# One filter load moved in the DMA queue, one Newton chain on another engine, more output buffers: a spectral mixer with token MLP, forward and backward

## The chip, the cores and the metric

The kernel runs on one core of one Trainium2 chip. The metric is the device time of one execution in microseconds (us), lower is better. A core has five engines that work at the same time, each through its own queue of instructions in order: TensorE (PE in the profile; its weight loads are PEld), VectorE (DVE), ScalarE (ACT), GpSimd (POOL) and SyncE (SP). In this kernel SP issues every DMA transfer.

## The reference

A pre-norm block on x of 2048 tokens by 448 features, and the gradients of everything:

```python
h  = x + irfft2(rfft2(layernorm(x)) * (w_r + 1j * w_i))       # over tokens and features
h2 = h + transpose(gelu(layernorm(h)^T @ w1 + b1) @ w2 + b2)  # an MLP over the tokens
_out, _vjp = jax.vjp(_f, A_x, A_w_r, A_w_i, B_w1, B_b1, B_w2, B_b2)
_grads = _vjp(grad_out)
```

w1 is 2048 by 1792, w2 is 1792 by 2048, and the two filters w_r and w_i are 2048 by 225. Outputs are h2 and the gradients of x, both filters, both weight matrices and both biases.

## The kernel before

All big arrays stay in on-chip memory in named regions (`rA`, `rB`, ..., `rX`); a region is used for one thing after another. Small helper classes hand out buffers: a `Ring` is a list of views used in turn, and `Ring.next()` first issues a store that is still put off for the view it hands out. `defer(us, fn, views)` puts a DMA off by a number of microseconds of planned TensorE work. The order of the instructions on TensorE, VectorE, ScalarE and SP is the order in which the program writes them; GpSimd's alone is chosen by a scheduler. `evac`, which copies a matmul's result out, is given to ScalarE or VectorE by a planner's running sum of costs when the kernel is built.

**Stages.** The Fourier transforms are matrix products with sine and cosine tables that the kernel makes itself.

1. Rows of x (loop over 16 row tiles t, the loop `for t in range(NT)` near L860). `ln_stats` gives mean and variance of a tile, a Newton iteration gives the inverse square root (`rstd_x`), `scale_R` multiplies a small transform matrix by it, `fold_prep` adds and subtracts mirrored halves of two tiles, `row_a` and `row_b` are the two products of the transform. Every second tile ends with a reshuffle (the deferred DMA of L655 in `row_b`), which carries 226 KB from the partitions of the row layout to those of the column layout, `D2`. Eight reshuffles are made; the second transform needs all of them.
2. `s2_stage`, the transform over tokens: per group g three forward matmuls on `D2`, a complex product with the filter on VectorE (`w_mult`), three inverse matmuls (`s2_inv`). Six pairs of groups lie between a forward matmul and its inverse. The filter is loaded in raw form by `w_load` in eight transfers, four for w_r and then four for w_i (L571), and `w_place` copies it into place while the stage runs. The first transfer of each has 64 partitions by 3600 elements, 450 KB.
3. `inv_rows`, the transform back, with the second layer norm.
4. The MLP, its backward pass, then the same transforms backward with the two weight gradients as filling.

**Filling.** While a stage waits for other engines, TensorE is given matmuls of another product: `fill(n)` takes n matmuls from `pending`. In stages 1 and 2 this is `dg_gen`, w2 times the output gradient, in 14 blocks j of 16 matmuls. Each block needs a transposed load of w2 (`load_w2T`, L294, a DMA transpose into one of five buffers, three in `rE` and two in `rO`). Blocks 8 and later are held back and issued in `fwd_x(0)`, the start of stage 2, from a list of kinds: T is a held w2 transpose, W is the next filter transfer.

**Rows 4 and 5.** The inverse deviations of rows 0 to 3 come from ScalarE and VectorE. For rows 4 and 5 `newton_gp` (L844) writes ten GpSimd operations on 128 by 2 elements; the later groups, rows 6 to 15, use the same function from inside the loop. `newton` (L353) is the same iteration as a list of nine VectorE operations, wrapped by `rstd_of(a, b)`, which nothing called.

**The last stage.** The two weight gradients are made by `gw_gen` (L1203), first for w2 (14 blocks, right operand `goT` in `rG`), then for w1 (16 blocks). Two blocks at a time, two output buffers of 1024 columns each are taken twice, filled by four evictions and stored by a DMA each. All of them come from one ring, `ost` (L1200), of six buffers in `rO`. They are the filling of the backward transforms; what is left of them runs at the very end, after `inv_rows`. The gradient of x is stored row tile by row tile (L1293), that of the filters by `g_out` (L560), all on SP's one queue.

Of the kernel before, what the change touches and what calls it, by code (L numbers as in the profile page):

```python
# [17 lines left out]
P = 128  # L18
S = 2048
# [79 lines left out]
class Ring:  # L99
# [7 lines left out]
    def next(self):  # L107
        v = self.views[self.i % len(self.views)]
        self.i += 1
        Ring.release(v)  # L110
        return v
# [8 lines left out]
def kernel(  # L120
# [20 lines left out]
    nc = tc.nc  # L141
# [14 lines left out]
    def region(name, n):  # L156
        return mem.tile([P, n], BF16, name=name)

    def cut(reg, off, *dims):
        n = int(np.prod(dims))  # L160
        v = reg[:, off:off + n]
        if len(dims) == 1:
            return v
        names = "abcd"[:len(dims)]
        return v.rearrange("p (" + " ".join(names) + ") -> p " + " ".join(names),
                           **{c: d for c, d in zip(names, dims)})

    def ring(reg, off, count, *dims):
        n = int(np.prod(dims))
        return Ring([cut(reg, off + i * n, *dims) for i in range(count)])  # L170
# [57 lines left out]
    rG = region("rG", 4 * S)  # L228
# [34 lines left out]
    rstd_x = mem.tile([P, NT], F32, name="rstd_x")  # L263
# [4 lines left out]
    mvx = mem.tile([P, NT, 2], F32, name="mvx")  # L268
# [20 lines left out]
    def load_w2T():  # L289
        j = w2T_ring.i  # L290
        if j == NFB:
            return
        wT = w2T_ring.next()
        nc.sync.dma_start_transpose(out=wT, in_=B_w2[j * P:(j + 1) * P, :].rearrange("f (t c) -> f t c", c=P))  # L294
        w2Ts.append(wT)
# [57 lines left out]
    def newton(v, y, sl):  # L353
        vi, yi = nt_i[:, 0, sl], y.bitcast(I32)
        a = nt_f[:, 0, sl]
        ops = []
        d = Later(ve, ops)
        d.tensor_scalar(out=v, in0=v, scalar1=LN_EPS, scalar2=None, op0=ALU.add)
        d.tensor_scalar(out=vi, in0=v.bitcast(I32), scalar1=1, scalar2=None, op0=ALU.arith_shift_right)
        d.tensor_scalar(out=yi, in0=vi, scalar1=-1.0, scalar2=RSQRT_MAGIC, op0=ALU.mult, op1=ALU.add)  # L360
        for c0, c1 in RSQRT_STEPS:
            d.tensor_tensor(out=a, in0=y, in1=y, op=ALU.mult)
            d.scalar_tensor_tensor(out=a, in0=a, scalar=c0, in1=v, op0=ALU.mult, op1=ALU.mult)
            d.scalar_tensor_tensor(out=y, in0=a, scalar=c1, in1=y, op0=ALU.add, op1=ALU.mult)
        return ops

    def newton_gp(v, y, sl):
        vi, yi = nt_i[:, 0, sl], y.bitcast(I32)
        a = nt_f[:, 0, sl]
        gp_.tensor_scalar(out=v, in0=v, scalar1=LN_EPS, scalar2=None, op0=ALU.add)  # L370
        gp_.tensor_scalar(out=yi, in0=v.bitcast(I32), scalar1=-0.5, scalar2=RSQRT_MAGIC, op0=ALU.mult, op1=ALU.add)
        for c0, c1 in RSQRT_STEPS:
            gp_.tensor_tensor(out=a, in0=y, in1=y, op=ALU.mult)
            gp_.tensor_tensor(out=a, in0=a, in1=v, op=ALU.mult)
            gp_.tensor_scalar(out=a, in0=a, scalar1=c0, scalar2=c1, op0=ALU.mult, op1=ALU.add)
            gp_.tensor_tensor(out=y, in0=a, in1=y, op=ALU.mult)
# [374 lines left out]
    def fill(n):  # L751
        while n > 0 and pending:
            try:
                next(pending[0])
                n -= 1
            except StopIteration:
                pending.pop(0)
# [5 lines left out]
    def ln_stats(src, t, mv):  # L763
        ve.bn_stats(out=stats[:, t, :], in_=src[:, t, :])
        if t % 2:
            ve.bn_aggr(out=mv[:, t - 1, :], in_=stats[:, t - 1, :])
        if t % 2:
            ve.bn_aggr(out=mv[:, t, :], in_=stats[:, t, :])
# [30 lines left out]
    def rstd_of(a, b):  # L799
        return newton(mvx[:, a:b, 1], rstd_x[:, a:b], slice(a, b))  # L800
# [40 lines left out]
    fold_prep(xn, 1)  # L841
    for t in (4, 5):
        ln_stats(xn, t, mvx)
    newton_gp(mvx[:, 4:6, 1], rstd_x[:, 4:6], slice(4, 6))  # L844
    fill(6)
    turn_biases = load_biases()
    Meter.side, Meter.every, Meter.count = [], 1, 0
# [3 lines left out]
    for c in range(2):  # L851
        sc.copy(out=Rp.rearrange("p (a q b c) -> p c a q b", c=2, q=8, a=4)[:, c],
                in_=Rm[:, 64 * c:64 * c + 64].rearrange("p (q a b) -> p a q b", q=8, a=4))
    FILL_A = (3, 3, 3, 3, 3, 3, 3, 3, 3, 3, 3, 3, 3, 3, 3, 3)
    FILL_B = (3, 3, 3, 3, 3, 3, 3, 3, 3, 3, 3, 3, 3, 3, 3, 3)
    for t in range(NT):
        if t in (1, 3):
            load_w2T()
        if t + 1 < NT:
            row_a(t + 1, Rs.pop(t + 1))  # L860
        fill(FILL_A[t])
        if 1 <= t and t + 3 < NT:
            if t + 3 in (4, 8, 12):
                while Meter.side:
                    Meter.side.pop(0)()
            Rs[t + 3] = scale_R(t + 3)
        row_b(t - 1)
        if t == NT - 1:
            row_b(t)
        if t % 2 and t < 12:  # L870
            fold_prep(xn, t // 2 + 2)
        for i in STATS.get(t, ()):
            ln_stats(xn, i, mvx)
        for _ in range(3 if t > 0 else 0):
            if next(uv, None):
                break
        if t in GROUPS:
            a, b = GROUPS[t]
            newton_gp(mvx[:, a:b, 1], rstd_x[:, a:b], slice(a, b))
        for _ in range((9, 10, 11, 12).count(t)):  # L880
            next(w_loads)
        if t in INV_S:
            gen_inv_s(INV_S[t])
        if t in (13, 13 + 1):
            gen_neg((cut(r448, NG * P, 12, P), cut(rE, 3 * NT * P, 4, P))[t - 13], Ut[:, 12 * (t - 13):12 + 4 * (t - 13), :])
        if t == 2:
            gen_RT()
        fill(FILL_B[t])
# [5 lines left out]

    def fwd_x(c2):
        if c2 == 0:
            for kind in "TWWWWTTT":
                if kind == "W":
                    next(w_loads)
                elif held_w2:  # L900
                    held_w2.pop(0)()
            cap[0] = NFB
            while held_w2:
                held_w2.pop(0)()
        if c2 == 4:
            turn_biases()
        return Xs[:, 2 * c2:2 * c2 + 2, :, :]
# [256 lines left out]
    for t in range(NT):  # L1164
# [6 lines left out]
        pb, tmp, m1, m2, _ = ln_a(t, pdh[:, 0:D], rstd_h[:, t:t + 1], hln[:, t, :], (1.0 + LN_EPS) / D)  # L1171
# [28 lines left out]
    ost = ring(rO, 0, 6, S // 2)  # L1200
    o4 = out_4.rearrange("(p t) f -> p t f", t=NT)

    def gw_gen(n, rhs, width, store):  # L1203
        for u in range(n // 2):
            st = ahead.pop(0)

            def whole(pw, w, c, i, k, start, stop):
                mm(pw[i][:, 0:w], lhsT=st[:, 4 * i + k, :], rhs=rhs(c, k, 0, P), start=start, stop=stop)

            def parts(pw, w, c, start):  # L1210
                for i in range(2):
                    mm(pw[i][:, 0:w], lhsT=st[64 * i:64 * i + 64, 3, :], rhs=rhs(c, 3, 64 * i, 64 * i + 64),
                       start=start, stop=not start)

            def out(pw, w, c, i):
                o = os_[i]
                x = c % 2 * 512
                evac(out=o[:, x:x + w], in_=pw[i][:, 0:w])
                if x:
                    if c == 3 and i:  # L1220
                        st_load()
                    defer(1.5, lambda j=2 * u + i: store(j, 512 * (c - 1), x + w, o), o)

            for c in range(0, 4, 2):
                os_ = [ost.next(), ost.next()]
                pw = [ps_mm(), ps_mm()]
                for i in range(2):
                    for k in range(3):
                        whole(pw, 512, c, i, k, k == 0, False)
                        yield  # L1230
                w = min(512, width - 512 * (c + 1))
                pv = [ps_mm(), ps_mm()]
                parts(pw, 512, c, False)
                parts(pv, w, c + 1, True)
                for i in range(2):
                    out(pw, 512, c, i)
                yield
                yield
                for i in range(2):
                    for k in range(3):  # L1240
                        whole(pv, w, c + 1, i, k, False, k == 2)
                        if k == 2:
                            out(pv, w, c + 1, i)
                        yield

    pending.append(gw_gen(NFB, lambda c, k, a, b: goT[a:b, k, c * 512:(c + 1) * 512], S,
                          lambda j, a, n, o: nc.sync.dma_start(out=out_6[j * P:(j + 1) * P, a:a + n], in_=o[:, 0:n])))
    pending.append(gw_gen(NT, lambda c, k, a, b: du_t[a:b, 4 * c:min(NFB, 4 * c + 4), k, :], F,
                          lambda t, a, n, o: nc.sync.dma_start(out=o4[:, t, a:a + n], in_=o[:, 0:n])))
    nc.sync.dma_start(out=rC[:, 0:NG * 2 * KW], in_=w_d[:])  # L1250
    for t in range(NT - LAG, NT + 2):
        if t == NT - 2:
# [78 lines left out]
```

## Time and profile before

| | us |
|---|---|
| median of four runs | 369.52 |
| lowest and highest | 368.38, 369.76 |
| the profiled execution | 369.76 |
| its span | 368.0 |
| granted TensorE clock, mean | 0.994 of full |
| idle before TensorE's matmuls in rows 0 to 15 and the transform over tokens, longest after the start | 1.69, 1.40, 1.19 |

The span is the stretch from the first to the last recorded instruction; what lies around it is 1.76 us. A line of the timeline gives the start, the length, the engine, the source line, the operation, what it writes and reads, the number of instructions that are merged, and in brackets how long the engine stood before it and what ended that. The two helper lines, L215 (every matmul) and L79 (every planned vector or scalar operation), stand for many places in the program, so one goes by the names of the tiles.

### The profile page before, as it was taken

Reading aid. Unit: us, or ns where it says so; the run is one execution under the profiler, and the core shown is the slowest. Engines: PE = TensorE matmul, PEld = TensorE weight load, DVE = VectorE, ACT = ScalarE, POOL = GpSimd, SP = SyncE. Lnnn points to the kernel's source line nnn. Section 1 sums busy time; section 2 is a strip of 40 time slices with the busy share of each in tenths; the row PEclk is TensorE's granted clock in tenths of the full one; section 3 lists DMA queues with packets and bytes.
Section 4 is the critical chain, followed back from the end, with each engine's and each line's share of the span. In section 5 each row is a group of like instructions: output and inputs, shape, how many; then the busy total and the mean of one; then the engine's idle time right before and its main releaser. Section 6 shows DMA issues by size and latency. Waiting matters only on the chain.

```text
span 368.0 us, 6387 instructions
## 1 busy us (share of the span) xinstructions
PE 344.3 (94%) x2114; PEld 185.3 (50%) x2121; DVE 255.6 (69%) x641; ACT 203.7 (55%) x426; POOL 73.6 (20%) x240
## 2 busy tenths in 40 slices
PE   1888998898999999999999999999999999999993
PEld 0455765555645555555555566653445444544541
DVE  7698839963866888683247766674787873688881
ACT  3748737866966544413312455453577664576761
POOL 8867000000220000010002222100000000465660
PEclk9999999999999999999999999999999999999997
DMA  8999999749999999797859698479768899798997
GB/s 208 306 189 224 185 199 165 155 146 298 291 302 348 322 300 251 187 288 166 211 137 183 152 183 161 91 226 311 209 201 228 251 183 253 236 204 273 198 211 237
DMA packets 148249, 81.63 MB, mean 222 GB/s; under 512 B 95544, under 2 KB 140600, under 8 KB 147832
## 3 DMA queue, kind: packets, MB, share of 16 engines
q1 hardware_dynamic: 148216, 81.23, 90.7%
q8 instruction: 16, 0.26, 0.3%
q14 instruction: 17, 0.14, 0.1%
HBM read 27.56 MB, written 23.89 MB: 140 GB/s over the span
## 4 chain that ended last, share of the span: by engine, by line
PE 77%; ACT 5%; POOL 5%; DMA 4%; DVE 4%; issue 3%; POOLq 0%; DVEq 0%; ACTq 0%
PE ps_mm L215 62%; PE ps_ff L215 15%; DMA out_dram<-rO 2%; DMA rO<-in_B_w_dram 2%; ACT rO L79 2%; ACT rG L79 1%; DVE r L79 1%; ACT Ut L79 1%; DVE stats L79 1%; DVE rO L79 1%; DVE rA L79 1%; POOL cols L394 1%; POOL cols L395 1%; ACT rAT L79 0%; ACT rX L79 0%
## 5 line engine op out<-in xcount | busy, mean ns | idle before, releaser
L215 PEld LDWEIGHTS <-r 128*128 128x128 bf16 (+1 forms) x628 | 60.2, 105 | 50.1 <-issue 2.7
L215 PEld LDWEIGHTS <-rS 128*128 128x128 bf16 (+2 forms) x528 | 44.3, 98 | 49.7 <-issue 9.5
L79 ACT CAST rO<-ps_mm 128x512 bf16<-128x512 f32 (+1 forms) x75 | 40.3, 567 | 25.2 <-PE ps_mm L215 22.0
L1130 POOL TENSOR_SCALAR lcol<-lcol 128x1 f32<-128x1 f32 x32 | 18.1, 565 | 148.6 <-ACT r L79 148.4
L215 PE MATMUL ps_mm<-rD,r 128*128 128x448 bf16 x224 | 44.5, 352 | 0.0
L79 DVE CAST rO<-ps_mm 128x512 bf16<-128x512 f32 (+1 forms) x45 | 28.4, 644 | 19.9 <-PE ps_mm L215 14.9
L215 PEld LDWEIGHTS <-rst 128*128 128x128 bf16 (+1 forms) x320 | 24.0, 97 | 29.0 <-issue 13.2
L215 PE MATMUL ps_mm<-rC,rE 128*128 128x448 bf16 x144 | 35.5, 365 | 0.9 <-DMA rE<-in_B_w_dram 0.5
L215 PE MATMUL ps_mm<-rG,rst 128*128 128x512 bf16 (+1 forms) x155 | 34.0, 380 | 0.2
L79 ACT CAST r<-ps_ff 128x452 bf16<-128x452 f32 x54 | 28.9, 538 | 9.4 <-PE ps_ff L215 9.2
L215 PE MATMUL ps_mm<-rB,r 128*128 128x448 bf16 x160 | 31.2, 352 | 0.1
L215 PE MATMUL ps_mm<-r,rst 128*128 128x512 bf16 (+3 forms) x160 | 31.3, 353 | 0.0
L79 ACT ACTIVATE r<-ps_mm,rstd_h 128x448 bf16<-128x448 f32 x16 | 10.1, 634 | 29.3 <-PE ps_mm L215 29.3
L215 PE MATMUL ps_ff<-csI,rAT 113*128 113x448 bf16 x108 | 24.9, 353 | 0.4 <-ACT rAT L79 0.2
L79 DVE SCALAR_TENSOR_TENSOR r<-ps_mm,b2col,r 128x448 bf16<-128x448 f32 x16 | 10.9, 682 | 19.9 <-PE ps_mm L215 18.2
L79 ACT ACTIVATE r<-rC 128x448 bf16<-128x448 bf16 x16 | 9.1, 572 | 26.7 <-DMA out_dram<-r 21.8
L79 ACT ACTIVATE rG<-rG 128x896 bf16<-128x896 bf16 x14 | 13.3, 950 | 14.9 <-DVE rG L79 14.7
L215 PEld LDWEIGHTS <-rO 128*128 128x128 bf16 (+1 forms) x165 | 15.5, 98 | 11.9 <-DMA rO<-in_B_w_dram 1.5
L215 PE MATMUL ps_mm<-rE,rS 128*128 128x448 bf16 x112 | 21.5, 352 | 0.0
L215 PE MATMUL ps_mm<-rC,rO 128*128 128x448 bf16 x80 | 19.1, 352 | 1.2 <-DMA rO<-in_B_w_dram 1.2
L79 ACT CAST rS<-ps_ff 128x512 bf16<-128x512 f32 x30 | 17.7, 590 | 4.2 <-PE ps_ff L215 4.2
L215 PE MATMUL ps_ff<-csF,rS 112*128 112x226 bf16 x128 | 17.7, 260 | 1.7 <-ACT rS L79 1.7
(173 smaller groups left out, 600.9 us busy)
## 6 DMA issues: line engine op xcount, KB each, us to landing
out_dram<-rO SPq DMA_DIRECT2D x44, 256.0 KB
r<-in_B_w_dram SPq DMA_DIRECT2D x5, 1024.0 KB
r<-r SPq DMA_DIRECT2D x16, 226.0 KB
r<-r SPq DMA_DIRECT2D x32, 113.0 KB
rS<-in_B_w_dram SPq DMA_DIRECT2D x4, 896.0 KB
out_dram<-r SPq DMA_DIRECT2D x32, 112.0 KB
out_dram<-rO SPq DMA_DIRECT2D x16, 192.0 KB
rO<-in_B_w_dram SPq DMA_DIRECT2D x2, 1024.0 KB
```

Of the source, the lines that this page charges most:

```text
L79: fn(**kw)
L215: nc.tensor.matmul(out, lhsT=lhsT, rhs=rhs, start=start, stop=stop)
L394: gp_.tensor_scalar(out=gtmp, in0=in0, scalar1=scalar, scalar2=None, op0=ALU.mult)
L395: gp_.tensor_tensor(out=out, in0=gtmp, in1=in1, op=ALU.add)
L1130: gp_.tensor_scalar(out=m1, in0=ms, scalar1=-1.0 / D, scalar2=None, op0=ALU.mult)
```

## The change

Three edits:

- The Newton iteration of rows 4 and 5 (the first two of its kind) is written with `rstd_of(4, 6)`, nine VectorE operations, in place of `newton_gp`. They stand on VectorE directly after the statistics of these rows and before those of rows 6 and 7.
- The first transfer of w_i is issued in the row loop at t = 15, and no longer as the first W of `fwd_x(0)`. The reshuffle of the last two rows is deferred at that point, so in SP's order the transfer comes to stand before that reshuffle, with block 8's transpose after both; the other three transfers stay where they were. In the list of kinds there is one W less.
- `gw_gen` takes its ring as an argument. The first gradient keeps the six buffers in `rO`. The second gets 14: eight in `rG`, whose old content `goT` is no longer needed then, followed by the six.

The instructions of TensorE and ScalarE are the same in number, kind and order (some write to `rG` in place of `rO`). VectorE gets nine more, GpSimd ten fewer.

```diff
@@ -841,7 +841,8 @@
     fold_prep(xn, 1)
     for t in (4, 5):
         ln_stats(xn, t, mvx)
-    newton_gp(mvx[:, 4:6, 1], rstd_x[:, 4:6], slice(4, 6))
+    for fn in rstd_of(4, 6):
+        fn()
     fill(6)
@@ -877,7 +878,7 @@
-        for _ in range((9, 10, 11, 12).count(t)):
+        for _ in range((9, 10, 11, 12, 15).count(t)):
             next(w_loads)
@@ -894,7 +895,7 @@
     def fwd_x(c2):
         if c2 == 0:
-            for kind in "TWWWWTTT":
+            for kind in "TWWWTTT":
                 if kind == "W":
                     next(w_loads)
@@ -1200,7 +1201,7 @@
     ost = ring(rO, 0, 6, S // 2)
...
-    def gw_gen(n, rhs, width, store):
+    def gw_gen(n, rhs, width, store, ost):
@@ -1244,9 +1245,10 @@
     pending.append(gw_gen(NFB, lambda c, k, a, b: goT[a:b, k, c * 512:(c + 1) * 512], S,
-                          lambda j, a, n, o: nc.sync.dma_start(out=out_6[j * P:(j + 1) * P, a:a + n], in_=o[:, 0:n])))
+                          lambda j, a, n, o: nc.sync.dma_start(out=out_6[j * P:(j + 1) * P, a:a + n], in_=o[:, 0:n]), ost))
     pending.append(gw_gen(NT, lambda c, k, a, b: du_t[a:b, 4 * c:min(NFB, 4 * c + 4), k, :], F,
-                          lambda t, a, n, o: nc.sync.dma_start(out=o4[:, t, a:a + n], in_=o[:, 0:n])))
+                          lambda t, a, n, o: nc.sync.dma_start(out=o4[:, t, a:a + n], in_=o[:, 0:n]),
+                          Ring(ring(rG, 0, 8, S // 2).views + ost.views)))
```

## The prediction

> **What bounds the kernel now.** I read the page first (busy shares, slices), then the chain of waits in order of time, then the three places that the change touches in the timeline of each engine, and last SP's own queue.
>
> ```profile
> PE 344.3 (94%) x2114; PEld 185.3 (50%) x2121; DVE 255.6 (69%) x641; ACT 203.7 (55%) x426; POOL 73.6 (20%) x240
> PE   1888998898999999999999999999999999999993
> PE 77%; ACT 5%; POOL 5%; DMA 4%; DVE 4%; issue 3%; POOLq 0%; DVEq 0%; ACTq 0%
> ```
>
> TensorE is busy 94% and its slices are full from about 70 us on; the losses are in the first 70 us and in the last slice, and only there can the change win anything.
>
> Place A, row 4 (timelines of VectorE and TensorE; start, length, then what ended the idle time):
>
> ```profile
> 15.55 0.30 DVE L79 BATCH_NORM_AGGREGATE mvx<-stats 128x2 f32<-128x6 f32 x2
> 18.77 0.26 DVE L79 TENSOR_SCALAR rX<-Rm,rstd_x 128x128 bf16<-128x128 bf16 x1 [2.92 <-POOL rstd_x L376]
> 19.38 0.64 PE L215 MATMUL ps_ff<-rX,rS 128*128 128x128 bf16 x4 [1.40 <-DVE rS L79]
> 30.19 0.56 PE L215 MATMUL ps_ff<-csF,rS 112*128 112x226 bf16 x4 [1.69 <-ACT rS L79]
> ```
>
> VectorE stands 2.92 us for row 4's inverse deviation, which GpSimd finishes at 18.75. After that VectorE is busy nearly without a gap (9.97 of 10 us between 20 and 30), the chain of waits runs POOL, DVE, ACT (the casts to `Ut`), and comes to TensorE at 30.19; from there TensorE runs on to 58.77.
>
> Place B, the filter loads (SP's queue, and TensorE):
>
> ```profile
> 44.39 2.63 SPq L655 DMA_DIRECT2D r<-r  x2
> 47.11 2.88 SPq L294 DMA_TRANSPOSE rO<-in_B_w_dram  x1
> 50.04 2.34 SPq L571 DMA_DIRECT2D rB<-in_A_w_i_dram  x4
> 52.48 4.82 SPq L294 DMA_TRANSPOSE rO<-in_B_w_dram  x1
> 59.96 0.55 PE L215 MATMUL ps_mm<-rC,rO 128*128 128x448 bf16 x2 [1.19 <-DMA rO<-in_B_w_dram]
> ```
>
> The transpose of block 9 of w2, issued at 52.48 behind four filter loads, lands late and TensorE stands 1.19 us. But look at what ends this stage:
>
> ```profile
> 79.89 0.70 DVE L79 TENSOR_TENSOR rS<-rS 128x452 bf16<-128x452 bf16 x2
> 80.65 0.36 PE L215 MATMUL ps_ff<-rS,VTt 128*128 128x452 bf16 x1
> ```
>
> VectorE makes its last product at 80.59 and TensorE's next inverse matmul starts 0.06 us later. From 57.02 to 80.59 the VectorE timeline shows no idle time before an instruction; its last wait is 0.39 us at 56.28, on ScalarE's `csI` casts, which wait for TensorE's transposes at 54.74, before the 1.19 us stall.
>
> Place C, the end:
>
> ```profile
> 361.61 0.86 ACT L79 CAST rO<-ps_mm 128x512 bf16<-128x512 f32 x2 [1.57 <-PE ps_mm L215]
> 362.63 1.02 DVE L79 CAST rO<-ps_mm 128x512 bf16<-128x512 f32 x2 [3.13 <-DMA out_dram<-rO]
> 364.26 0.81 SPq L1249 DMA_DIRECT2D out_dram<-rO  x2
> ```
>
> The last VectorE evictions wait for a store to free its `rO` buffer. TensorE ends at 361.91.
>
> **What the Trainium skill says.** "VectorE: DVE Perf Modes", section on the TRN2 errata, says that a VectorE operation pays a fixed cost whatever its size, about 150 cycles at 0.96 GHz as measured there; the trace agrees (a 128x2 reciprocal and the 128x2 aggregates take 0.16 to 0.18 us). "GPSIMD Engine Reference", 4.1, puts elementwise work on VectorE; here GpSimd's 128x2 steps show 0.19 us and 0.08 us of issue after them, so size matters little on either. "DMA: Bandwidth & Descriptors", section on queues, rings and completion order, says that each DMA engine takes the descriptors of one issuing queue in ring order: a load put ahead of a reshuffle is served ahead of it. The trace agrees so far as block 9's issue took 4.82 us behind the loads and block 8's 2.88 us without them.
>
> **Part A: the chain moves to VectorE.** Removed: 10 GpSimd operations, interleaved with others up to 18.75. Added: 9 VectorE operations of 128x2, each waiting for the one before, right after the aggregates of rows 4 and 5 (end 14.5). Their price is not in the trace; the nearest step is the reciprocal of 128x2 at 7.48, followed by its dependent at 7.68: 0.20 us. Bounds: 0.14 us (the operation alone) to 0.33 us (the dependent 128x16 step at 22.48). I take 0.20, so 1.8 us. The statistics of rows 6 and 7 behind them then end at 15.77 + 1.8 = 17.6 in place of 15.77, and row 4's scaling starts at 17.6 in place of 18.77: 1.2 us earlier (1.7 to 0 by the bounds). TensorE is free at 17.98 and gets row 4's fold 0.6 us after the scaling, at 18.2: its 1.40 us wait falls to 0.2. Row 5's scaling at 21.78 and the `Ut` chain follow VectorE, so 30.19 becomes 29.0. GpSimd starts the chain of rows 6 and 7 at 17.6 and needs 10 x 0.275 = 2.75 us, done at 20.4; it is wanted at 23.16 - 1.2 = 22.0, so that wait is covered. If GpSimd's order puts row 8's first step ahead of row 6's last, that step waits only for the aggregates at about 19.5.
>
> Does the 1.2 us survive? SP issues without a pause to 38.98 and then waits to 41.06: 2.1 us of room, more than 1.2. From there SP's reshuffles and transposes are released by evictions, so they move with it. From 105.6 to 199 TensorE has no wait at all, and loads are released by its own progress. I carry 1.2 us to the end.
>
> **Part B: one filter load ahead of the last reshuffle.** Nothing is added; one issue of about 0.585 us (2.34 / 4) moves ahead of the last reshuffle (of the two in the 2.63 us line the first takes its start and the second its end, about 0.59 us each: 46.43 to 47.02) and block 8's transpose. SP stands idle between the two last reshuffles (45.0 to 46.4), so the issue is hidden there. Its 450 KB are queued ahead: at the 238 GB/s of 52 to 54 us, 1.9 us, of which some runs while the reshuffle before is still moving. What waits behind: the last reshuffle, wanted by TensorE at 50.26, and block 8, wanted at 52.99; neither shows a wait now. DMA moves at 290 GB/s from 50.1 to 51.9 (that is block 8), so block 8 has about 1.0 us to spare. I take no new stall, bound 0 to 1.5. The gain: block 9 is issued 0.59 us sooner with half of the loads before it, so the 1.19 us stall goes. But VectorE's unbroken work from 57 to 80.59 does not begin sooner for that, and TensorE merely comes earlier to wait for it. Worth 0.06 to 0.1; I take 0.1. If TensorE's stall did hold the stage, it would be 1.2.
>
> **Part C: 14 buffers for the last output.** The operations are the same on every engine, only names change; `rG`'s readers (the products of the first weight gradient) stand earlier in TensorE's order. Waits on an `out_dram<-rO` store add up to 4.4 us in three places in the last stage, two of them in the last 10 us. TensorE is not held by them (32 matmuls need 12,544 columns / 2400 = 5.2 us, they took 5.9 from 356.02). So only the finish counts: VectorE's last two evictions could start when ScalarE's do, 361.61 for 362.63, 1.0 us earlier; but SP is busy to 363.81 with the stores before, so the last two stores go out at about 363.85 for 364.26. That is 0.4, and with a little less queue ahead I take 0.5 (bounds 0 and 1.0). The DMA engines are at 0.95 of full share from 352 to 366, so more is not to be had.
>
> **Sum.** 1.2 + 0.1 + 0.5 = 1.8 us off the profiled execution's 369.76 (span 368.0 and 1.76 around it) gives 367.96. That execution lies 0.24 above the median of the runs, 369.52; against the median I forecast 367.7.
>
> **Rivals.**
> - The VectorE chain costs as much as the wait that it removes: 9 x 0.33 = 2.97 against 2.92. For it: every step waits for the one before, and the only dependent step of similar kind in that stretch took 0.33. Against: that one writes 16 integers a row. Then A is 0, and 369.52 - 0.6 = 368.9. Chance 0.20.
> - Block 9's stall does hold the stage, and B pays in full: 1.1 more, 366.6. For it: TensorE's later waits (0.89 and 0.33 near 67 us) are on ScalarE, not on VectorE. Against: the 0.06 us at 80.65. Chance 0.11.
> - Slower: the filter load holds up the last reshuffle and block 8. If it keeps the queue for 2.7 us (half of the 5.5 us that about 900 KB took from 52 to 57.5) and there is no spare time, TensorE stands 2.7 us at the start of the transform: 2.7 - 1.7 = 1.0 slower, 370.5. It decides from a delay above 1.7 us on. For it: block 9 took 7.4 us from issue to use with loads ahead, block 8 at most 5.9. Against: the load has over a microsecond's start on the reshuffle. Chance 0.12.
> - The forecast: 0.57.
>
> **How the numbers follow.** About 0.3% (1.1 us: 368.4 and 370.6) is what a measurement can tell from no change. The forecast case alone spans 366.7 to 368.9 by the bounds of A and C; about 0.49 of its 0.57 lies under 368.4. With the whole of the second rival that makes faster 0.60; the first rival and the rest of the forecast give same 0.28, with part of the slower case; slower keeps 0.12 with all of its weight near 370.6. The range reaches from the second rival's 366.6, a little below, to 370.0, leaving out most of the slower case.
>
> **What would show it.** A: the scaling of row 4 starts near 17.6 and waits for no GpSimd step; nine 128x2 operations of about 0.20 us stand before it; TensorE's 30.19 becomes 29.0. B: the wait on `rO<-in_B_w_dram` is gone, and in its place TensorE waits for VectorE or ScalarE between 60 and 81, with the VectorE product's end still 0.1 before TensorE's inverse matmul. A wait at the first transform matmul (50.26 now) or at block 8 proves the slower rival. C: no wait on `out_dram<-rO` in the last 10 us, and the last store about 0.4 earlier against TensorE's end. I am wrong if TensorE's gain at 30 us is lost again before 105, or if the end gains a full microsecond.

## The result, and the profile after

The changed kernel took 370.74 us (median of 40 runs, 368.39 to 374.88) beside 368.79 us (61 runs) for the kernel before on the same chip. The ratio is 1.0046, with a 95% interval of 1.0032 to 1.0061: about 1.7 us slower, where I had forecast 1.8 us faster. Runs over 1.5% above the fastest of their kernel are left out of every ratio; of the changed kernel's 41, with the profiled one, 38 are compared. The profiled execution took 372.7 us, its span is 370.9; it is one of the longer ones, and the section on the fillers comes back to that.

The page of the changed kernel, with the same three rows as shown of before and the row of the granted TensorE clock in the place of TensorE's slices:

```profile
PE 347.7 (94%) x2114; PEld 186.3 (50%) x2121; DVE 256.6 (69%) x650; ACT 203.6 (55%) x426; POOL 71.0 (19%) x230
PEclk9999979999999999999999999999999999999998
PE 80%; DVE 8%; ACT 5%; issue 2%; DMA 2%; POOL 2%; ACTq 0%; DVEq 0%; POOLq 0%
```

The same 2114 matmuls were busy 3.4 us longer (347.7 for 344.3), and the clock row has a 7 in its sixth slice, which begins at 46 us. TensorE ran slower for a while just where the filter load was moved, which no part of the forecast contains.

Place A, VectorE's timeline of the changed kernel (start, length, what is written and read, and in brackets the idle time ahead of it):

```profile
13.22 0.30 DVE L79 BATCH_NORM_AGGREGATE mvx<-stats 128x2 f32<-128x6 f32 x2
13.56 0.17 DVE L79 TENSOR_SCALAR mvx<-mvx 128x2 f32<-128x2 f32 x1
13.76 0.17 DVE L79 TENSOR_SCALAR nt_i<-mvx 128x2 int32<-128x2 int32 x1
...
15.14 0.16 DVE L79 SCALAR_TENSOR_TENSOR rstd_x<-nt_f,rstd_x 128x2 f32<-128x2 f32 x1
15.22 1.15 DVE L79 BATCH_NORM_STATS2 stats<-rA 128x6 f32<-128x448 bf16 x2
16.29 0.30 DVE L79 BATCH_NORM_AGGREGATE mvx<-stats 128x2 f32<-128x6 f32 x2
16.50 0.22 DVE L79 TENSOR_SCALAR rX<-Rm,rstd_x 128x128 bf16<-128x128 bf16 x1
```

The nine steps follow each other every 0.20 us, and row 4's scaling starts without the 2.92 us wait. It starts 2.27 us earlier than in the profile before (16.50 for 18.77), of which 1.08 us is not the change: in this execution TensorE's first matmul already starts at 6.91 instead of 7.99, on the first rows of x. The change itself is worth 1.2 us here.

Place B, TensorE's timeline of the changed kernel:

```profile
27.88 0.56 PE L215 MATMUL ps_ff<-csF,rS 112*128 112x226 bf16 x4 [1.70 <-ACT rS L79]
...
51.66 0.54 PE L215 MATMUL ps_ff<-r,Vt 128*128 128x452 bf16 x1 [3.55 <-DMA r<-r]
...
52.37 1.33 PE L215 MATMUL ps_mm<-rC,rE 128*128 128x448 bf16 x3
...
74.57 0.36 PE L215 MATMUL ps_ff<-rS,VTt 128*128 128x452 bf16 x1 [0.63 <-DVE rS L79]
```

At 27.88 TensorE is still 2.31 us ahead of the kernel before (30.19). At the first matmul of the token transform, where the kernel before had no wait at 50.26, it stands 3.55 us for the last reshuffle (`r<-r` is L655's DMA) and is 1.40 us behind. The three filling matmuls after it took 1.33 us; the same three took 0.73 before. The 1.19 us wait on block 9 is gone, and the later waits are on VectorE.

SP's own queue in the changed kernel (start of the issue, time on SP):

```profile
42.67 0.59 SPq L571 DMA_DIRECT2D rB<-in_A_w_i_dram  x1
44.17 0.55 SPq L655 DMA_DIRECT2D r<-r  x1
44.81 6.46 SPq L294 DMA_TRANSPOSE rO<-in_B_w_dram  x1
51.33 1.71 SPq L571 DMA_DIRECT2D rB<-in_A_w_i_dram  x3
53.14 3.36 SPq L294 DMA_TRANSPOSE rO<-in_B_w_dram  x1
```

The load goes out 1.5 us ahead of the last reshuffle, and the transpose of block 8 right behind it keeps SP for 6.46 us, where before it took 2.88. The instruction is the same, so I read the length of its issue as a rough gauge of how much lies in the queue; over the runs below it is 4.87 to 6.85 us with 450 KB more ahead of it, and 2.22 to 3.95 without. The chain of waits prices the reshuffle (start, length, what):

```profile
44.17 7.35 DMA r<-r
```

7.35 us from issue to use, where the kernel before, which issues it at 46.49, had at most 50.26 - 46.49 = 3.77 for it. The trace also holds every DMA packet with its start, its length and its size. The load is 64 packets of 7200 bytes, a reshuffle 128 of 1808. The load, issued at 42.67, has its first packet at 46.29: it stands in line for 3.6 us. Of its 64 packets 57 then run between 46.25 and 48.25, with the DMA engines full, and only after that comes the bulk of the last reshuffle, whose last packet ends at 51.04. In the kernel before it ends at 49.21.

Then the clock, in one-microsecond stretches of the changed kernel (columns: TensorE's busy time, with the number of matmuls, the granted clock, the share of the DMA engines, GB/s):

```profile
49.00:50.00 1.00, 0.00 (x0) 1.00 1.07 186
50.00:51.00 1.00, 0.00 (x0) 0.69 1.82 113
51.00:52.00 1.00, 0.34 (x2) 0.50 0.88 188
52.00:53.00 1.00, 1.00 (x5) 0.50 1.53 285
...
57.00:58.00 1.00, 1.00 (x7) 0.90 1.08 245
```

The clock is halved at about 50.4 (a slice mean of 0.69 is 0.38 us at full and 0.62 at half) and is full again at 57.2, so the stage's first 5.5 us run at half speed. This brings the second set of VectorE's `csI` steps, from which on VectorE is busy without a pause, from 56.28 to 60.38: 4.1 us late.

Place C, the end of the changed kernel:

```profile
364.28 1.26 DVE L79 CAST rG<-ps_mm 128x512 bf16<-128x512 f32 x2 [1.60 <-PE ps_mm L215]
...
367.26 0.81 SPq L1250 DMA_DIRECT2D out_dram<-rG  x2
```

The last VectorE evictions no longer wait for a store but for their matmuls. TensorE ends at 365.08, 5.8 us before the span does; in the kernel before it was 6.1.

### The profile page after: what moved, and what is told of

It is laid out like the page before. It is cut to its first block, busy times and chain, and to the rows that moved or that the text cites. A ratio compares the mean times of both kernels' runs of the same rounds, so it can differ in the third digit from the quotient of the medians.

```text
span 370.9 us, 6356 instructions
## 1 busy us (share of the span) xinstructions
PE 347.7 (94%) x2114; PEld 186.3 (50%) x2121; DVE 256.6 (69%) x650; ACT 203.6 (55%) x426; POOL 71.0 (19%) x230
## 4 chain that ended last, share of the span: by engine, by line
PE 80%; DVE 8%; ACT 5%; issue 2%; DMA 2%; POOL 2%; ACTq 0%; DVEq 0%; POOLq 0%
PE ps_mm L215 64%; PE ps_ff L215 15%; DMA r<-r 2%; ACT rO L79 2%; DVE rS L79 2%; DVE r L79 2%; DVE rG L79 1%; DVE stats L79 1%; DVE rX L79 1%; ACT Ut L79 1%; ACT L79 1%; DVE rA L79 1%; POOL nt_f L374 0%; ACT r L79 0%; ACT rAT L79 0%
## 5 line engine op out<-in xcount | busy, mean ns | idle before, releaser
L215 PE MATMUL ps_mm<-rC,rE 128*128 128x448 bf16 x144 | 37.2, 377 | 1.8 <-DMA rE<-in_B_w_dram 1.3
L79 ACT CAST rO<-ps_mm 128x512 bf16<-128x512 f32 (+1 forms) x52 | 28.5, 582 | 14.9 <-PE ps_mm L215 11.7
L79 DVE CAST rO<-ps_mm 128x512 bf16<-128x512 f32 (+1 forms) x28 | 18.1, 657 | 11.8 <-PE ps_mm L215 11.8
L215 PEld LDWEIGHTS <-rE 128*128 128x128 bf16 x148 | 14.5, 103 | 11.0 <-issue 3.1
```

What stands on the lines that cost most here:

```text
L79: fn(**kw)
L215: nc.tensor.matmul(out, lhsT=lhsT, rhs=rhs, start=start, stop=stop)
```

## The experiments

All ratios are to the kernel before, run on the same chip in the same session.

### Without the moved load

Against the changed kernel:

```diff
-        for _ in range((9, 10, 11, 12, 15).count(t)):
+        for _ in range((9, 10, 11, 12).count(t)):
...
-            for kind in "TWWWTTT":
+            for kind in "TWWWWTTT":
```

> The Newton chain on VectorE and the 14 output buffers are kept; the filter load goes back to its place behind the last reshuffle. If the filter load ahead of the reshuffle is the cause (theory), the first matmul of the token transform waits for no reshuffle or for less than 0.5 us, the granted clock stays at 1.00 from 50 to 60 us, and the time is 1.2 + 0.4 = 1.6 us below the kernel before, ratio about 0.9957. If the gain of the Newton chain would be lost in any case, because the last reshuffle cannot come earlier than the kernel before has it (rival), TensorE waits some 1.2 us or more for the reshuffle even here, and the time is only 0.4 us below before, ratio about 0.999. If the buffers or the chain themselves cost time elsewhere, the ratio is above 1.

Measured: 368.58 us, ratio 0.9984, interval 0.9968 to 1.0000. TensorE's timeline of this kernel:

```profile
28.96 0.56 PE L215 MATMUL ps_ff<-csF,rS 112*128 112x226 bf16 x4 [1.70 <-ACT rS L79]
...
49.82 0.35 PE L215 MATMUL ps_ff<-r,Vt 128*128 128x452 bf16 x1 [0.63 <-DMA r<-r]
```

Without the moved load the loss is gone, the clock stays at 1.00, and the kernel is about 0.6 us faster than before, but not 1.6. This execution begins like the one of before (first matmul at 7.99), so the two can be compared directly: TensorE is 1.23 us ahead at 28.96 and only 0.44 ahead at 49.82, since it now waits for the same reshuffle. So both theories hold in part: the loss goes with the load, and more than half of the Newton chain's gain is lost at the reshuffle even without it.

### The moved load alone

On the kernel before:

```diff
-        for _ in range((9, 10, 11, 12).count(t)):
+        for _ in range((9, 10, 11, 12, 15).count(t)):
...
-            for kind in "TWWWWTTT":
+            for kind in "TWWWTTT":
```

> Only the filter load is moved ahead of the last reshuffle; Newton chain and buffers are as before. Theory (the load in the queue holds up the reshuffle): TensorE stands 1.5 to 3 us at the first matmul of the token transform, now 1.2 us less than in the changed kernel because it comes later to it, and if the wait passes some 2 us the clock falls as well; time 2 to 4 us above before, ratio 1.005 to 1.011. Rival (the load only hurts together with the earlier arrival of TensorE there): no wait or one under 0.5 us, ratio 1.000 to 1.001.

Measured: 371.13 us, ratio 1.0050, interval 1.0027 to 1.0072, and in TensorE's timeline of it:

```profile
52.40 0.35 PE L215 MATMUL ps_ff<-r,Vt 128*128 128x452 bf16 x1 [1.97 <-DMA r<-r]
```

The load alone makes the whole loss; it needs no earlier TensorE. Here the wait is 1.97 us and the clock stays full in the profile. The load's packets begin at 47.04, 2.1 us after its issue, and the last reshuffle's end at 51.75.

### The load behind the reshuffle

On the kernel without the moved load:

```diff
-            for kind in "TWWWWTTT":
+            for kind in "WTWWWTTT":
```

> As the first experiment, but the first w_i load is issued directly behind the last reshuffle and still ahead of block 8's transpose, so that against the changed kernel only the order of this load and the last reshuffle is exchanged. If the order of the two is what counts (theory), the wait at the first matmul of the transform falls under 1 us and the time is that of the first experiment within 0.5 us, ratio about 0.996 to 0.997, unless block 8 then comes late: that would show as a wait on the w2 transpose in rO near 50 us. If the bytes of the load crowd the reshuffle wherever they stand (rival), the wait stays near 3 us and the ratio near 1.004.

Measured: 368.87 us, ratio 0.9993, interval 0.9973 to 1.0014. TensorE's timeline:

```profile
50.57 0.35 PE L215 MATMUL ps_ff<-r,Vt 128*128 128x452 bf16 x1 [2.45 <-DMA r<-r]
```

The time lies with the theory, well under the changed kernel's, but the interval doesn't separate it from the first experiment. The wait does not: the profiled execution stood 2.45 us. It had begun 1.08 us early (first matmul at 6.92), so a usual one would stand about 1.4. The load behind the reshuffle costs less than the load ahead of it, and not nothing: the reshuffle's last packet ends at 49.59, 0.4 us later than in the first experiment, and TensorE starts 0.98 us after that packet, where it starts 0.62 after it there.

### The clock kept up, with 18 and with 8 filling matmuls

```diff
     fill(20)
+    keep = ps_ff()
+    for _ in range(18):
+        mm(keep[:, 0:D], lhsT=ident[:], rhs=go_tp[:, 0, :], start=True, stop=True)
```

> The changed kernel with 18 matmuls of 448 columns more ahead of the token transform, 3.4 us of work whose result nothing reads, so that TensorE is busy in the stretch in which it waits for the last reshuffle. Computation is added and nothing left out. If the fall of the clock to half between 50 and 57 us is caused by that idle stretch and costs time of its own (theory), the clock stays at 1.00, the token transform starts where it does in the changed kernel or up to 0.3 us later, and the time is 1.5 to 3 us below the changed kernel, ratio to before about 0.997 to 1.001. If the clock falls for another reason, or the slower clock is hidden behind VectorE (rival), the time is that of the changed kernel or a little more, ratio 1.004 to 1.006.

Measured: 371.23 us, ratio 1.0049, interval 1.0031 to 1.0067. TensorE's timeline:

```profile
48.81 3.57 PE L215 MATMUL ps_ff<-rC,ident 128*128 128x448 bf16 x18
52.22 0.39 PE L215 MATMUL ps_ff<-permI,Vt 128*128 128x128 bf16 x4
52.58 0.35 PE L215 MATMUL ps_ff<-r,Vt 128*128 128x452 bf16 x1
```

The clock stayed at 1.00, no run has a mean clock under 0.994, and TensorE did not wait for the reshuffle at all. The ratio is nevertheless the one that I had given to the rival. The fillers cost little by outlasting the reshuffle: its last packet ends at 51.93, and after the 0.6 us that lie between packet and start in the other profiles TensorE could have started near 52.5. Why the runs are no faster than the changed kernel's stays open. The same with `range(8)`:

> The changed kernel with 8 matmuls of 448 columns more ahead of the token transform, 1.5 us, so that they end before the last reshuffle lands (18 of them ended after it and so cost time of their own). Nothing is left out. Theory: the granted clock falls only where TensorE stands more than about 2.5 us; with 8 fillers it stands 1 to 2 us at most, the mean clock of every run is at 0.994 or above as in the 24 quicker ones of the changed kernel's 41 runs (median 369.93 us), and the median comes near 370, ratio to before about 1.002 to 1.003, so 0.5 to 1 us below the changed kernel. Rival: the clock is a symptom of a late reshuffle and costs nothing itself, since VectorE sets this stage; then the ratio stays at 1.004 to 1.006.

Measured: 369.73 us, ratio 1.0023, interval 1.0010 to 1.0037; the mean clock of all 22 runs is at 0.995 or above. TensorE's timeline:

```profile
52.24 0.35 PE L215 MATMUL ps_ff<-r,Vt 128*128 128x452 bf16 x1 [2.18 <-DMA r<-r]
```

Eight useless matmuls, 1.5 us of work, make the changed kernel faster. They don't bring the reshuffle sooner (its last packet ends at 51.59, for 51.04 in the changed kernel), so of the loss some 0.0046 - 0.0023 = 0.0023, or 0.85 us, was the halved clock. By the two intervals this size is rough, anything from about 0.1 to 1.6 us. The changed kernel's own runs say the same: of the 38 that are compared, 14 had a mean clock under 0.994 and a median of 371.61 us, the other 24 a median of 369.93. A longer wait also lengthens these runs, so the 1.7 us between them is not the clock's alone.

The profiles price the clock without the wait. From the first matmul of the transform to the first of the MLP it is 52.6 to 53.3 us in the ten profiles with a full clock there (52.65 with 8 fillers, 104.89 less 52.24), and 55.1 to 55.6 in the four in which it was halved (55.32 in the changed kernel, 106.98 less 51.66; one of the four also has a long wait in the stage). An execution in which the clock falls thus loses about 2.4 us. If it fell in the 14 of 38, that is 0.9 us on average, which agrees with the fillers.

### The bytes ahead of the reshuffle: 7 KB, and 450 KB less

The transfer that goes ahead is now the smallest of w_i. In `w_load` the four transfers of w_i are turned so that the last comes first; the rest is as in the changed kernel:

```diff
-            for p0, p1, j0, j1, row, dims in ((0, 64, 0, 16, 0, [[16 * DF, 4]]), (64, 112, 0, 16, 97, [[-16 * DF, 3]]),
-                                              (112, 128, 0, 15, 113, []), (112, 128, 15, 16, 64, [])):
+            parts = ((0, 64, 0, 16, 0, [[16 * DF, 4]]), (64, 112, 0, 16, 97, [[-16 * DF, 3]]),
+                     (112, 128, 0, 15, 113, []), (112, 128, 15, 16, 64, []))
+            for p0, p1, j0, j1, row, dims in (parts[3:] + parts[:3] if c_ else parts):
```

> The changed kernel, but the w_i transfer that goes ahead of the last reshuffle is the one of 7 KB; the one of 450 KB follows first behind block 8's transpose. The number of transfers ahead is that of the changed kernel, only the bytes are 64 times fewer. Theory (bytes in the queue): the wait at the first matmul of the transform falls to that of the first experiment, about 0.6 us, and the ratio to 0.998 to 0.999. Rival (a transfer of another kind ahead of the reshuffle, its issue or its place in the rings, is what costs): the wait stays at 2 us or more and the ratio at 1.003 to 1.005.

Measured: 368.14 us, ratio 0.9983, interval 0.9965 to 1.0001.

```profile
50.10 0.35 PE L215 MATMUL ps_ff<-r,Vt 128*128 128x452 bf16 x1 [0.91 <-DMA r<-r]
```

One transfer more in the same place, with 7 KB in place of 450, costs nothing that can be seen. It is the bytes and not the place or the issue.

The opposite step, on the kernel without the moved load: w_r's transfers are turned too (`parts[1:] + parts[:1]` for w_r), and its 450 KB one goes behind block 8's transpose:

```diff
-        for _ in range((9, 10, 11, 12).count(t)):
+        for _ in range((9, 10, 11).count(t)):
...
-            for kind in "TWWWWTTT":
+            for kind in "TWWWWWTTT":
```

> The first experiment's kernel with the opposite step: here a 450 KB load of the real filter, which in all other kernels stands ahead of the last reshuffles, is issued behind the last reshuffle and block 8's transpose, with the w_i loads. Theory (the DMA queue is full up to the transform, and every byte put ahead of the last reshuffle delays it): the reshuffle lands up to 1.9 us sooner than in the first experiment, the 0.63 us wait there is gone, and 0.3 to 0.6 us more are won, ratio 0.997 to 0.998. In exchange block 9's transpose comes later, and TensorE's wait there grows from 1 us to 2 to 3 us. If that wait counts (my rival of the prediction, in which block 9 holds the stage), the ratio is above 1.001.

Measured: 370.63 us, ratio 1.0033, interval 1.0013 to 1.0053. TensorE's timeline, and then one line of VectorE's:

```profile
48.14 0.35 PE L215 MATMUL ps_ff<-r,Vt 128*128 128x452 bf16 x1
...
59.37 0.55 PE L215 MATMUL ps_mm<-rC,rO 128*128 128x448 bf16 x2 [2.71 <-DMA rO<-in_B_w_dram]
```

```profile
63.92 0.63 DVE L79 CAST rX<-ps_ff 128x452 bf16<-128x452 f32 x1 [2.66 <-PE ps_ff L215]
```

The first half of the theory holds: with 450 KB less ahead of it the reshuffle is there when TensorE comes at 48.14, and there is no wait; its last packet ends at 46.93, and the DMA engines even ran half empty before it (a share of 0.42 and 0.45 at 44 to 46 us). The second half falls. Block 9's transpose now comes 8.95 us after its issue, TensorE stands 2.71 us in the middle of the stage, the clock is halved again (from 60.0 to 63.4 us), and VectorE runs dry for 2.66 us. The stage is bound by VectorE only as long as TensorE keeps feeding it; a wait of 1.2 us there is hidden, one of 2.7 us and a half clock are not.

### Newton chain alone, buffers alone

The first hunk of the change on the kernel before:

```diff
-    newton_gp(mvx[:, 4:6, 1], rstd_x[:, 4:6], slice(4, 6))
+    for fn in rstd_of(4, 6):
+        fn()
```

> The kernel before with the Newton chain of rows 4 and 5 on VectorE and nothing else. By my prediction's step A: 1.2 us, ratio 0.9967. By what the first experiment showed: TensorE comes to the transform 1.1 us earlier and waits there some 0.6 us for the last reshuffle, so 0.5 us, ratio 0.9985 to 0.999.

Measured: 368.99 us, ratio 1.0002, interval 0.9983 to 1.0020.

```profile
28.97 0.56 PE L215 MATMUL ps_ff<-csF,rS 112*128 112x226 bf16 x4 [1.70 <-ACT rS L79]
...
49.66 0.35 PE L215 MATMUL ps_ff<-r,Vt 128*128 128x452 bf16 x1 [0.46 <-DMA r<-r]
```

Again 1.22 us at 28.97, and 0.60 left at 49.66. The time shows none of it, but the interval is too wide to rule out 0.6 us; it does rule out the 1.2 of my step A.

The buffers alone are the third hunk of the diff (the ring as an argument of `gw_gen`, and the ring of 14 for the second gradient), with the first two undone:

> The kernel before with the 14 output buffers for the last gradient and nothing else. By my prediction's step C: the last stores go out 0.4 to 0.5 us earlier, ratio 0.9987. Rival: the first experiment's gain of 0.6 us is all the Newton chain's, and the buffers give nothing, ratio 0.9995 to 1.0005. In the profile, from TensorE's last matmul to the end of the span it is 6.1 us in the kernel before: 5.6 to 5.8 by the first, 6.1 by the rival.

Measured: 368.93 us, ratio 1.0000, interval 0.9983 to 1.0017. From TensorE's last matmul (361.64) to the end of the span it is 5.9 us. Over all profiles this stretch is 5.6 to 6.4 us in the eleven with 14 buffers, and 5.8, 6.1 and 6.6 in the three with six. If the buffers give anything it is 0.2 us or so, and it can't be told from nothing.

### The load earlier still

On the changed kernel:

```diff
-        for _ in range((9, 10, 11, 12, 15).count(t)):
+        for _ in range((9, 10, 11, 12, 13).count(t)):
```

> The changed kernel with the 450 KB filter load issued two row tiles earlier still, at t = 13, ahead of the last two or three reshuffles. If the load only has to be out of the last reshuffle's way (rival), it is done when that one is issued, the wait is at most that of the first experiment, 0.6 us, and the ratio 0.998. If the DMA queue is behind all the way, so that every byte ahead of the last reshuffle delays it wherever it stands (theory), the wait stays between 1.5 and 3.5 us and the ratio between 1.002 and 1.005.

Measured: 371.14 us (370.33 without one run of 728.84, which the ratio leaves out), ratio 1.0055, interval 1.0024 to 1.0085.

```profile
52.06 0.54 PE L215 MATMUL ps_ff<-r,Vt 128*128 128x452 bf16 x1 [3.93 <-DMA r<-r]
```

The load is now issued at 39.44, in the pause of SP that I had called room, and 3.2 us sooner than in the changed kernel. It doesn't help: the load's first packet runs at 45.79, 6.4 us after its issue, and the last reshuffle's last at 51.43. The queue has no room when SP has. The rival falls.

### The last reshuffle on another queue

On the changed kernel, and in the second run on the kernel without the moved load:

```diff
-            defer(RESH_LAG, lambda: nc.sync.dma_start(out=D2[u:u + 121:8]
+            defer(RESH_LAG, lambda: (nc.scalar if u == NT // 2 - 1 else nc.sync).dma_start(out=D2[u:u + 121:8]
```

> The changed kernel, filter load at t = 15 included, but the last reshuffle is issued on ScalarE's queue and not on SP's. If it is held up by standing behind the load in one queue's order (theory of the rings), it overtakes the load and lands within about 4.5 us of its issue, the wait falls under 1 us and the ratio to 0.997 to 0.999. If it is held up because the 16 engines share their bandwidth among all that is queued (rival, for which the 2.45 us wait with the load behind it speaks), the wait stays at 2 us or more and the ratio at 1.002 to 1.005.

Measured: 374.29 us (5 runs), ratio 1.0145, interval 1.0120 to 1.0171.

```profile
55.64 0.56 PE L215 MATMUL ps_ff<-r,Vt 128*128 128x452 bf16 x1 [6.45 <-DMA r<-r]
```

> The first experiment's kernel with the last reshuffle on ScalarE's queue, the version that could beat both. If the queue's order matters, the reshuffle does not wait behind the two before it, the 0.63 us wait goes, and the ratio is 0.995 to 0.997. If the bandwidth is what counts, it is the first experiment's, 0.998 to 0.999. ScalarE loses some 0.6 us for the issue near 45 us, where it has room.

Measured: 370.81 us, ratio 1.0037, interval 1.0019 to 1.0056.

```profile
51.04 0.35 PE L215 MATMUL ps_ff<-r,Vt 128*128 128x452 bf16 x1 [1.84 <-DMA r<-r]
```

This profile is of a run of 368.32 us, 2.5 us under the median, so its 1.84 us may not be a usual wait.

Both are worse than with SP's queue, and both by more than either theory allowed. The edit did more than change the queue: as SP no longer waits to issue the reshuffle, block 8's transpose goes out at 43.80 or 44.43, ahead of the reshuffle at 45.26. In the first run the filter load and this transpose are both in flight ahead, and the reshuffle took 10.34 us; in the second the transpose alone, and it took 5.63, beside 4.42 on SP's queue with the transpose behind it. So in these two runs another queue didn't let a late transfer overtake what was already on its way.

## Why the prediction was wrong, step by step

The start of the transform in eight of the kernels, by the bytes that stand ahead of the last reshuffle (with the end of the reshuffle's last packet, and the reshuffle's time from its issue to its use from the chains of waits):

| ahead of the last reshuffle | kernels | TensorE starts the transform, us | last packet ends, us | issue to use, us |
|---|---|---|---|---|
| 450 KB less | w_r load moved behind | 48.14, no wait | 46.93 | |
| as before | without the moved load; Newton alone; 7 KB ahead | 49.82, 49.66, 50.10 | 49.20, 49.01, 49.48 | 4.42, 4.26, 4.71 |
| 450 KB more | changed; load alone; 8 fillers; load earlier | 51.66, 52.40, 52.24, 52.06 | 51.04, 51.75, 51.59, 51.43 | 7.35, 5.77, 7.49, 7.73 |

The third column hardly depends on when the reshuffle was issued: in the last row the issues lie 2.3 us apart (44.17 to 46.50) and the starts 0.7. It depends on the bytes: 450 KB more move it by 2.2 us (the means of the two rows), which is about 200 GB/s and a usual rate of the DMA columns, and by the packets 450 KB less bring the reshuffle 2.3 us sooner. So the transfers run behind their issues here, and what counts is the amount of data that has to be moved until then. This explains B. Of A it explains only a part, as the packets show below.

**Part A: the chain was priced right, its survival wrong.** Nine steps of 0.20 us, the scaling 1.2 us earlier, and 29.0 at TensorE (28.96, 28.97 in the kernels that begin like before): all as forecast. The step that failed is "Does the 1.2 us survive?". I argued that SP has 2.1 us of room and that the reshuffles move with the evictions that release them. Their issues did (46.49 became 45.26); the landing of the last did not (its last packet ends at 49.21 before, and at 49.20 and 49.01 in the two kernels with the Newton chain and no moved load). Of 1.2 us about 0.4 to 0.6 is left at the start of the transform, and no timed run resolves even that. A full queue is not the whole reason. Without the moved load 112 of the 128 packets have started by 48.0, where the kernel before had 26; the last 16 follow one or two at a time up to 49.20, with a DMA share of 0.48 from 48 to 49. Why these few trail was not pulled apart. The absence of a wait at 50.26 had only shown that the reshuffle was not late, and I read it as spare time. With the 0.6 us from the last packet to TensorE's start in the kernels that wait, it was there about 0.4 us ahead.

**Part B: "I take no new stall, bound 0 to 1.5" is the term that turned the sign.** The runs show about 2.2 us of delay for the reshuffle. My slower rival had named this place and a price of 2.7 us, and I gave it 0.12, against it the load's start of over a microsecond. The start is real (1.5 us in the profile), but it would only help if the load could run in it; the DMA engines had the reshuffles before on their hands, and the load's first packet ran 3.6 us after its issue. In the kernel before the DMA share is 1.05 from 38 to 47 us, at only 182 GB/s. I had priced the load by GB/s of later stretches (238 and 290) and left out the share here, which was full: with the reshuffles the engines are busy at a low rate. The rival's 370.5 us comes near the measured 370.74 partly by luck, since it counted a gain of 1.7 us that the runs don't show and left out the clock.

The section on queues, rings and completion order of "DMA: Bandwidth & Descriptors" in the Trainium skill, from which I took that a load put ahead is served ahead, was right, and its next statement bears on the runs too: a transfer's completion is signalled by an ordered write that lands only after every earlier write of that DMA engine, across its queues. The two runs with ScalarE's queue agree: TensorE starts 1.04 and 1.27 us after the reshuffle's last packet there, and 0.62 to 0.65 after it in the seven kernels of the table that wait. Most of the 10.34 us is not this, though, since that last packet itself ends only at 54.60. The section of the same page on issuing engines says that transfers run on the same 16 engines and interleave whoever issues them, which fits the same two runs. Why a load behind the reshuffle still delayed it, by 0.4 us in the packets and as much from the last packet to the start, was not pulled apart; that is one execution, and stays open.

**The clock was in no step.** "TensorE: Matmul & The Clock Gate" in the Trainium skill, in its section on why this matters for kernels, warns of idle gaps above about 3 us; the trace shows such a fall, and sooner, after 2.3 us. My own slower rival had a stall of 2.7 us and I didn't ask what follows it. Of the changed kernel's 2.3 us against the kernel without the moved load (1.0046 less 0.9984), about 1.4 is the wait (1.0023 less 0.9984, the run with 8 fillers) and 0.85 the clock.

**The stage itself was read right.** Block 9's wait is gone, waits on ScalarE and VectorE are in its place, and the lost wait brought little, as forecast: from the start of the transform to the MLP it is 52.6 to 53.0 us in the four profiles at full clock without that wait, and 52.7 to 53.3 in the six with it. But "VectorE-bound" was a statement about small waits: a start 2 us later moves the end of the stage by nearly as much. With the load alone the transform begins 2.14 us later and the MLP's first matmuls 1.77 us later (105.36 for 103.59).

**Part C** removed its wait as forecast; the 0.4 to 0.5 us were too much. In the changed kernel SP's last stores still stand behind those of the filter gradient, and over all profiles the stretch from TensorE's end to the span's end is some 0.2 us shorter on average (5.9 for 6.2).

The best kernels of the study are the changed one without the moved load (0.9984) and the one with 7 KB moved (0.9983). They are about 0.6 us faster than before at the best estimate, with intervals that just reach no change.

## What to carry to other kernels

A transfer without a wait isn't a transfer with time to spare: before putting bytes ahead of it, read the share of the DMA engines (not the GB/s) over the stretch ahead of it. Where it was full, in these runs, 450 KB more ahead cost their whole 2.2 us, whether they were issued 1.5 or 4.8 us before the transfer. A gain on the engines ends at the next transfer that does not land sooner when it is issued sooner. And where a stall of TensorE may pass 2 us, price the slower clock after it as well, or give TensorE something to do.

## What the runs showed of the hardware that I had not expected

- The clock fell 2.3 us after TensorE's last matmul in the changed kernel (idle from 48.1, half speed from 50.4), 3.1 us after it with the load at t = 13 (48.1, 51.2), 4.7 us after it with the reshuffle on ScalarE's queue (49.2, 53.9), and 3.3 us after it with 450 KB taken from ahead (56.7, 60.0), where TensorE was already at work again for 0.6 us; all by the slices' mean clocks. Waits of 2.18 and 2.45 us passed without it. So a threshold of 2.5 us, as I had set it for the fillers, is not shown: whether a wait of 2 to 3 us costs the clock is not sure from one execution to the next, and this fits with the wider scatter of the kernels that wait.
- It stayed at half for 6.8 us three times (50.4 to 57.2, 51.2 to 58.0, 53.9 to 60.7), with TensorE standing during the first 0.9 to 1.8 us of it, and for 3.4 us where TensorE had begun again before the fall (60.0 to 63.4). The Trainium skill ("TensorE: Matmul & The Clock Gate", Part 1) gives about 3.4 us of sustained work for the return; here it was 5.1 to 6.0 us from TensorE's restart in the three, and 4.0 in the fourth.
- Executions begin in two ways, with the first matmul at 6.91 or at 7.99 us, in kernels that have the same code up to there, and TensorE's wait near 337 us is 0 in the profile without the moved load and 1.2 in the one with 7 KB moved, which have the same code there. Single profiles therefore differ by over a microsecond before a change has done anything, and a place is better compared by its waits, and between executions that begin alike.
